# Inverse transform's first products in eight array tiles: even and odd frequencies apart, two groups per block

## The chip, the cores and the metric

The kernel runs on one core of a Trainium2 chip. The time is device microseconds from the first to the last instruction of the core, with what lies around them, as a median over repeated runs. Five engines work side by side: TensorE (PE, with PEld for its weight loads), VectorE (DVE), ScalarE (ACT), GpSimd (POOL) and SyncE (SP), which only issues DMAs here.

## The reference

```python
# x: (8, 3008, 256), filters: (1505, 256), w_in: (256, 2048), w_out: (2048, 256), all float32
X = np.fft.rfft(x, axis=1)
Y = X * (filt_r + 1j * filt_i)[None, :, :]
y = np.fft.irfft(Y, n=3008, axis=1).astype(np.float32)
x = y.reshape(8 * 3008, 256)
h = x @ w_in
out = (h * (1.0 / (1.0 + np.exp(-h))) @ w_out).astype(np.float32)
```

A filter in the frequency domain along the 3008 tokens of each of 8 batches, and then a two-layer network with a SiLU between the layers, on all 24064 tokens.

## The kernel before

**Two kinds of work share TensorE.** The network is the larger one. A batch has 48 steps: 2 halves of the tokens, 3 pairs of chunks in each half (256, 256 and 240 columns), and 8 pairs of blocks of the hidden dimension (`jp`). Both layers multiply 2x2 blocks with seven products each instead of eight. `hidden(step)` makes the first layer (products into px and pyz, combined by ScalarE and VectorE, SiLU on ScalarE), and `project(step - 1)` makes the second layer one step later, into the four accumulator banks a0 to a3 of a pair of chunks. When the last `jp` of a pair is projected, `drain` copies the accumulators out: a0 and a2 on ScalarE, a1 and a3 on VectorE; POOL then makes seven additions, and VectorE's transposes and SP's stores follow some steps later (`output`).

**The transform of batch b** is done while batch b - 1 is in the network, in pieces put between the steps (`spectral`):

- `load_x`, `sums`, `stage1` (products pa, L284, and a store to DRAM by POOL), eight times.
- `load_t2` (SP), `forward` (products pb, L307, into two banks), six groups g of frequencies.
- `multiply` (filter, VectorE, L319) and `add` (L327, L328), into tiles z of 64 real and imaginary rows for each of two banks k.
- `inverse` (products pc, L337): tile z times the table e_t, 128 columns of outputs that stand for 64 values of n and two parts. Two copies (`evac`, alternately VectorE L208 and ScalarE L210) and four stores to DRAM (L348) follow at once.
- `load_t4` (SP) and `stage3` (products pd, L368), eight groups; the first four before the batch enters the network, and the last four during its steps 9 to 18. The copies of pd make the tile y that the network reads (`tokens` forms its sums and differences).

**Who sets the order.** The schedule is written out by hand. A step has eight rounds. In each round `hidden` and `project` each issue what belongs to it, at most one product each, and then the pieces whose time has come are issued: `put(step, rnd, piece)` gives a piece its step and round, and `plan(b)` names them relative to the batch's first step (`at`). Each engine executes its own instructions in the order of issue; SP's and POOL's DMA queues too. A tile's buffer is taken again only after its last reader.

**PSUM** has eight banks: px, pyz, two banks of the pool `fps` (tag f) for all transform products of batches 1 to 7, and a0 to a3. Batch 0, whose transform runs before the network starts, uses f and a0 to a3 in a ring of six (`bank`).

The order in which `project` uses the accumulators (operand, slot of g, accumulator i, half h of its bank):

```python
PROJECT = [(A11, 0, 0, 0), (A12, 3, 1, 0), (S4, 2, 2, 0), (S1, 4, 0, 1), (S3, 5, 1, 1),
           (S2, 6, 2, 1), (A22, 7, 3, 0)]
```

Batch 0's transform, the loading of filters and tables and the rounding of the network's weights (`round_weights`, L590 to L603) make up the start, before the first network product.

Of the kernel before, what the change touches and what calls it, by code (L numbers as in the profile page):

```python
# [36 lines left out]
FP32 = mybir.dt.float32  # L40
U32 = mybir.dt.uint32
AFT = mybir.ActivationFunctionType
ALU = mybir.AluOpType
# [6 lines left out]
NS, NG = 24, 6  # L50
# [35 lines left out]
def dft_tables():  # L86

    wf = np.zeros((128, 2, 64))
    for par in range(2):
        for i, idx in enumerate(ORDER):  # L90
            ph = 2 * np.pi * (np.arange(N1) * (2 * idx + par) % 94) / 94
            for h in range(2):
                wf[64 * h:64 * h + N1, par, 2 * i] = np.cos(ph)
                wf[64 * h:64 * h + N1, par, 2 * i + 1] = -np.sin(ph)


    d = np.zeros((2, 2, 32, NS, 2, 32))
    n = np.arange(32)[:, None]
    for par in range(2):
        for i, idx in enumerate(ORDER):  # L100
            sp = 2 * idx + par
            kap = kept(sp)
            sg = np.where((kap - sp) % 94 == 0, 1.0, -1.0)
            k = np.where((kap - sp) % 94 == 0, kap, S - kap)
            th = 2 * np.pi * (n * k % S) / S
            d[par, 0, :, i, 0], d[par, 1, :, i, 0] = np.cos(th), np.sin(th)
            d[par, 0, :, i, 1], d[par, 1, :, i, 1] = -np.sin(th) * sg, np.cos(th) * sg


    e = np.zeros((4, 32, NG, 2, 2, 2, N2))  # L110
    n = np.arange(N2)[None, :]
    for g in range(NG):
        for bank in range(2):
            for j in range(4):
                s = slot_residue(g, bank, j - j % 2)
                kap = kept(slot_residue(g, bank, j))
                sg = np.where((kap - s) % N1 == 0, 1.0, -1.0)[:, None]
                k = np.where((kap - s) % N1 == 0, kap, S - kap)[:, None]
                assert ((k - s) % N1 == 0).all()
                th = 2 * np.pi * (n * k % S) / S  # L120
                e[j, :, g, bank, 0, 0], e[j, :, g, bank, 0, 1] = np.cos(th), np.sin(th)
                e[j, :, g, bank, 1, 0], e[j, :, g, bank, 1, 1] = -np.sin(th) * sg, np.cos(th) * sg


    ph = 2 * np.pi * (np.outer(np.arange(N1), np.arange(NS)) % N1) / N1
    v = np.stack([2 * np.cos(ph), -2 * np.sin(ph)], 0)

    v[0, :, 0], v[1, :, 0] = 1.0, 0.0
    wi = np.zeros((128, N1))
    for h in range(2):  # L130
        wi[64 * h:64 * h + 2 * NS] = v.transpose(0, 2, 1).reshape(2 * NS, N1) / S
    f32 = np.float32
    return (wf.astype(f32), wi.astype(f32), d.reshape(128, NS, 2, 32).astype(f32),
            e.reshape(128, NG, 2, 2, 128).astype(f32))


@with_exitstack
def kernel(
# [18 lines left out]
    def pool(name, bufs, space=None):  # L157
        kw = {} if space is None else {"space": space}
        return ctx.enter_context(tc.tile_pool(name=name, bufs=bufs, **kw))
# [5 lines left out]
    upool = pool("u", 1)  # L165
    tpool = pool("t12", 2)
    ppool = pool("p", 2)
    zpool = pool("z", 3)
    qpool = pool("q", 2)
    t4pool = pool("t4", 2)  # L170
    gpool = pool("g", 2)
# [8 lines left out]
    wf_t = cpool.tile([128, 2, 64], FP32)  # L180
    wi_t = cpool.tile([128, N1], FP32)
    d_t = cpool.tile([128, NS, 2, 32], FP32)
    e_t = cpool.tile([128, NG, 2, 2, 128], FP32)
    f_t = [cpool.tile([128, NG, 2, C], FP32, name=f"filt{i}") for i in range(2)]

    w_t = cpool.tile([128, 7, 2, NJP, 128], FP32)
# [18 lines left out]
    def evac(dst, src):  # L205
        flip[0] ^= 1
        if flip[0]:
            nc.vector.tensor_copy(out=dst, in_=src)  # L208
        else:
            nc.scalar.copy(out=dst, in_=src)  # L210
# [1 line left out]
    y = {}  # L212
    early = [0]

    def bank(b, name):

        if b > 0 or early[0] is None:
            return fps.tile([128, 2, C], FP32, name=name, tag="f")
        early[0] += 1
        k = early[0] % 6  # L220
        if k < 2:
            return fps.tile([128, 2, C], FP32, name=name, tag="f")
        return accps.tile([128, 2, C], FP32, name=name, tag=f"a{k - 2}")

    def spectral(b):

        d1 = dpool.tile([2, NS, 2, 32, C], FP32, name=f"d1_{b}", tag="d1")
        d2 = dpool.tile([2 * NS, N2, C], FP32, name=f"d2_{b}", tag="d2")
        xs, us, t2s, banks, prods, t4s = {}, {}, {}, {}, {}, {}

        def load_x(u):

# [94 lines left out]
            eng.tensor_tensor(out=z[:, 0], in0=z[:, 0], in1=pt[:, 1], op=ALU.subtract)  # L327
            eng.tensor_tensor(out=z[:, 1], in0=z[:, 1], in1=pt[:, 0], op=ALU.add)  # L328

        def inverse(g):  # L330
            zs = [z for z, _ in prods.pop(g)]
            ps = [bank(b, f"pc_{b}_{g}_{i}") for i in range(2)]
            for k in range(2):
                for ri in range(2):
                    for i in range(2):
                        rows = slice(64 * i, 64 * i + 64)
                        nc.tensor.matmul(out=ps[i][:, k, :], lhsT=e_t[rows, g, k, ri, :],  # L337
                                         rhs=zs[k][rows, ri, :], start=(ri == 0), stop=(ri == 1))
            for i in range(2):
                if b > 0 or i == 0:  # L340
                    qt = qpool.tile([128, 2, C], FP32, name=f"q_{b}_{g}_{i}", tag="q")
                else:
                    qt = opool.tile([128, 2, C], FP32, name=f"q_{b}_{g}_{i}", tag="o")
                evac(qt, ps[i])
                for p in range(2):
                    a0 = p * NS + 2 * g + 12 * i
                    queue = nc.gpsimd if b > 0 or (g == NG - 1 and i == 0) else nc.scalar
                    queue.dma_start(out=d2[a0:a0 + 2, :, :].rearrange("s n c -> n s c"),  # L348
                                    in_=qt[64 * p:64 * p + 64, :, :])

        def load_t4(g):
            t4s[g] = t4pool.tile([128, 4, C], FP32, name=f"t4_{b}_{g}", tag="t4")
            for h in range(2):
                nc.sync.dma_start(out=t4s[g][64 * h:64 * h + 2 * NS],
                                  in_=d2[:, 32 * h + 4 * g:32 * h + 4 * g + 4, :])

        def stage3(g):
            half, n0 = divmod(4 * g, 16)
# [16 lines left out]
            for h in range(2):  # L375
                evac(dst[:, :, h, n0:n0 + 4], ps[h])

        return dict(load_x=load_x, sums=sums, stage1=stage1, load_t2=load_t2, forward=forward,
                    multiply=multiply, add=add, inverse=inverse, load_t4=load_t4, stage3=stage3)

    pending = []

# [4 lines left out]
    def plan(b, part):  # L387

        at = STEPS * b

        put(at - 51, 0, part["load_x"], 0)
        put(at - 51, 0, part["load_x"], 1)
        for u in range(8):
            put(at + u - (48 if u else 49), 5, part["sums"], u)
            put(at + u - 47, 3, part["stage1"], u)
        put(at - 39, 0, part["load_t2"], 0)
        put(at - 39, 0, part["load_t2"], 1)
        for g, step in enumerate((-37, -34, -31, -28, -25, -21)):
            late = 4 if g == 4 else 0
            put(at + step, 3, part["forward"], g)  # L400
            put(at + step, 5, part["multiply"], g, 0)
            put(at + step + 1, 1, part["multiply"], g, 1)
            put(at + step + 1, 5 + late, part["add"], g, 0)
            put(at + step + 2, 1 + late, part["add"], g, 1)
            put(at + step + (3 if late else 2), 3, part["inverse"], g)
        put(at - 18, 5, part["load_t4"], 0)
        for g, step in enumerate((-16, -12, -8, -4)):
            put(at + step, 3, part["stage3"], g)
        plan_rest(b, part)

    def plan_rest(b, part):
# [85 lines left out]
    def project(step):  # L497

        pair, jp = divmod(step, NJP)
        n, g = pairs[pair][3], g_t.pop(step)  # L500
        if jp == 0:
            acc[pair] = [accps.tile([128, 2, 256], FP32, name=f"acc_{pair}_{i}", tag=f"a{i}")
                         for i in range(4)]
        last = jp == NJP - 1
        for c, k, i, h in PROJECT:

            nc.tensor.matmul(out=acc[pair][i][:, h, 0:n], lhsT=w_t[:, c, 1, jp], rhs=g[:, k, 0:n],  # L507
                             start=(jp == 0 and h == 0), stop=last, skip_group_check=True)
            if last and (h == 1 or i == 3):
                drain(pair, i)  # L510
            yield
# [118 lines left out]
    def rounded(j):  # L630
        if wide:
            round_weights(j)
        else:
            load_exact(j)


    nc.sync.dma_start(out=wf_t, in_=wf_dram.ap())
    nc.gpsimd.memset(bias_t, -896.0)
# [17 lines left out]
    for g in range(NG):  # L656
        part["forward"](g)
        if g == 0:
            load_filters(4, 2 * NG)
            nc.sync.dma_start(out=wi_t, in_=wi_dram.ap())  # L660
        if g < 3:
            weights(1 + g)
        for k in range(2):
            part["multiply"](g, k)
        for k in range(2):
            part["add"](g, k)
        if 2 <= g < NG - 1:
            rounded(g)
        if g > 0:
            part["inverse"](g - 1)  # L670
    part["inverse"](NG - 1)
    weights(4)
    part["load_t4"](0)
    for j in range(5, 9):
# [74 lines left out]
```

## Time and profile before

| what | value |
|---|---|
| median of 3 runs | 2720.2 us (2719.74 to 2721.34) |
| profiled execution, its own time | 2718.15 us |
| its span, first to last instruction | 2716.4 us |
| mean granted TensorE clock | 0.987 |
| first network product starts | 126.6 us |
| TensorE / VectorE / ScalarE / POOL busy, 0 to 127 us | 57.1 / 75.0 / 24.5 / 57.9 us |
| the same, 184 to 2717 us | 2521.2 / 1531.1 / 1049.5 / 420.2 us |
| DMA share, 0 to 127 us, and 184 to 2717 us | 0.88, 0.23 |

TensorE's busy time is that of overlapping, pipelined matmuls with modelled ends: a busy TensorE is not one at its peak, and how long a block of matmuls occupies it is read from start times. Each fp32 matmul of the code is two records of matmul and two of weight load. In a group of the profile, the first number after the bar is the group's busy time in microseconds, the second the mean of one instruction in nanoseconds, and after the second bar stands the time its engine sat idle before it, with what ended that idle time. A timeline line has start and length in microseconds.

### The profile page before, as it was taken

To read this page: it belongs to the slowest core of one execution; us is meant where nothing else is said; L and a number is where in the kernel's file an instruction comes from. 1 tells how busy PE (TensorE), PEld (TensorE's weight loads), DVE (VectorE), ACT (ScalarE), POOL (GpSimd) and SP (SyncE) were. 2 spreads that over 40 slices of the span, in tenths; PEclk is the share of its full clock that TensorE was granted. 3 is DMA by queue.
4 is the path that set the end of the run, shared out by engine and by line. 5 is a ranking of instruction groups with operands and counts; after the bars stand their busy time and mean duration, and the time that the engine had idled before them with its cause. 6 is when DMAs were issued, how large, how long until landed. Compare 5 with 4: busy or idle time off the path is not lost.

```text
span 2716.4 us, 45798 instructions
## 1 busy us (share of the span) xinstructions
PE 2626.7 (97%) x17664; PEld 2203.4 (81%) x17664; DVE 1654.5 (61%) x3494; ACT 1099.1 (40%) x2994; POOL 505.1 (19%) x738
## 2 busy tenths in 40 slices
PE   4589999999999999999999999999999999999998
PEld 1368888788887888888887888978888788898987
DVE  4786655666566665666656665566655666555554
ACT  1244344433444334444444434444344443444443
POOL 3542111211011111111201121021111111100100
PEclk9699999999999999999999999999999999999999
DMA  9733121421224211332122312133121421110000
GB/s 216 191 101 86 40 47 31 107 63 37 43 59 99 61 43 24 81 88 53 36 44 77 80 44 55 29 97 70 39 47 43 102 65 35 37 28 21 9 16 16
DMA packets 188122, 166.95 MB, mean 61 GB/s; under 512 B 122432, under 2 KB 155584, under 8 KB 187648
## 3 DMA queue, kind: packets, MB, share of 16 engines
q1 hardware_dynamic: 166296, 111.89, 18.1%
q0 software_dynamic: 16352, 47.47, 6.9%
q10 hardware_dynamic: 5256, 4.67, 0.8%
q8 instruction: 138, 2.26, 0.3%
q14 instruction: 80, 0.66, 0.1%
HBM read 88.96 MB, written 74.97 MB: 60 GB/s over the span
## 4 chain that ended last, share of the span: by engine, by line
PE 93%; DMA 3%; DVE 2%; issue 1%; ACT 1%; SPq 0%; POOL 0%; ACTq 0%; DVEq 0%
PE acc L507 41%; PE px L451 25%; PE pyz L451 18%; PE pc L337 3%; PE pd L368 2%; PE pa L284 2%; PE pb L307 2%; DMA x<-in_x_dram 1%; DVE g L422 0%; DMA filt<-in_filt_i_dram 0%; DMA raw<-in_moe_w_out_dram 0%; DVE u L267 0%; DMA e_t<-e_tbl 0%; DMA d<-q 0%; DMA t<-d 0%
## 5 line engine op out<-in xcount | busy, mean ns | idle before, releaser
L507 PE MATMUL acc<-g,w_t 128*128 128x256 f32 (+1 forms) x5376 | 1513.3, 375 | 0.4 <-DVE g L422 0.4
L507 PEld LDWEIGHTS acc<-g,w_t 128*128 128x128 f32 x5376 | 1023.0, 190 | 114.8 <-DVE g L422 0.8
L422 DVE TENSOR_TENSOR g<-pyz,abc 128x256 f32<-128x256 f32 (+1 forms) x1152 | 479.3, 416 | 543.7 <-ACT abc L472 317.2
L422 DVE TENSOR_TENSOR g<-g 128x256 f32<-128x256 f32 (+3 forms) x1152 | 613.2, 532 | 196.7 <-ACT g L455 183.5
L451 PE MATMUL px<-ty,w_t 128*128 128x256 f32 (+1 forms) x2304 | 695.6, 384 | 4.0 <-ACT abc L466 3.5
L455 ACT ACTIVATE g<-g 128x256 f32<-128x256 f32 (+1 forms) x1152 | 472.9, 411 | 232.3 <-DVE g L422 232.3
L451 PEld LDWEIGHTS px<-ty,w_t 128*128 128x128 f32 x2304 | 421.1, 190 | 128.5 <-issue 71.9
L451 PE MATMUL pyz<-y,w_t 128*128 128x256 f32 (+1 forms) x1536 | 456.3, 379 | 1.7 <-DVE g L422 1.7
L422 POOL TENSOR_TENSOR s<-s 128x256 f32<-128x256 f32 (+1 forms) x329 | 263.0, 816 | 976.0 <-DVE s L525 952.8
L451 PEld LDWEIGHTS pyz<-y,w_t 128*128 128x128 f32 x1536 | 282.2, 190 | 46.9 <-DVE g L422 8.1
L466 ACT COPY abc<-px 128x256 f32<-128x256 f32 (+1 forms) x384 | 141.3, 368 | 375.1 <-PE px L451 375.1
L455 ACT ACTIVATE g<-px 128x256 f32<-128x256 f32 (+1 forms) x384 | 145.8, 380 | 301.2 <-PE px L451 301.2
L472 ACT COPY abc<-px 128x256 f32<-128x256 f32 (+1 forms) x384 | 142.9, 372 | 285.3 <-PE px L451 284.9
L348 POOL DMA_DIRECT2D d<-q x170 | 100.6, 598 | 755.7 <-DVE q L208 750.4
L451 PE MATMUL px<-y,w_t 128*128 128x256 f32 (+1 forms) x768 | 226.6, 377 | 3.6 <-ACT g L455 2.6
L451 PE MATMUL pyz<-ty,w_t 128*128 128x256 f32 (+1 forms) x768 | 226.7, 377 | 0.3 <-DVE g L422 0.3
L451 PEld LDWEIGHTS px<-y,w_t 128*128 128x128 f32 x768 | 144.6, 190 | 22.5 <-issue 3.0
L451 PEld LDWEIGHTS pyz<-ty,w_t 128*128 128x128 f32 x768 | 145.2, 190 | 19.5 <-DVE g L422 3.2
L459 ACT COPY abc<-px 128x256 f32<-128x256 f32 (+1 forms) x384 | 134.1, 349 | 1.3 <-PE px L451 1.3
L289 POOL DMA_DIRECT2D d<-t x124 | 63.5, 516 | 294.6 <-ACT abc L472 276.8
L208 DVE COPY y<-pd 128x376 f32<-128x376 f32 x64 | 51.4, 807 | 94.8 <-PE pd L368 94.8
L337 PE MATMUL pc<-z,e_t 64*128 64x256 f32 x768 | 102.7, 410 | 4.0 <-DMA e_t<-e_tbl 2.6
(52 smaller groups left out, 1316.4 us busy)
## 6 DMA issues: line engine op xcount, KB each, us to landing
t<-d SPq DMA_DIRECT2D x96, 256.0 KB, 3.9
t<-d SPq DMA_DIRECT2D x128, 192.0 KB, 3.7
d<-t POOLq DMA_DIRECT2D x124, 192.0 KB, 3.0
d<-q POOLq DMA_DIRECT2D x170, 128.0 KB, 2.6
out_dram<-o SPq DMA_DIRECT2D x636, 32.0 KB, 1.8
x<-in_x_dram SPq DMA_DIRECT2D x120, 128.0 KB, 3.1
x<-in_x_dram SPq DMA_DIRECT2D x120, 60.0 KB, 3.0
raw<-in_moe_w_in_dram SPq DMA_DIRECT2D x16, 256.0 KB, 4.8
```

What stands on the lines that cost most here:

```text
L284: nc.tensor.matmul(out=ps[h][64 * par:64 * par + 64], lhsT=wf_t[rows, par], rhs=ut[rows, par], start=True, stop=True)
L289: nc.gpsimd.dma_start(out=d1[par].rearrange("s p n c -> (s p) n c")[:, 4 * u:4 * u + 4, :], in_=t1[64 * par:64 * par + 2 * NS].rearrange(" ...
L307: nc.tensor.matmul(out=ps[k][32 * j:32 * j + 32, ri, :], lhsT=d_t[rows, 4 * g + at, ri, :], rhs=t2[rows, at, :], start=True, stop=True)
L337: nc.tensor.matmul(out=ps[i][:, k, :], lhsT=e_t[rows, g, k, ri, :], rhs=zs[k][rows, ri, :], start=(ri == 0), stop=(ri == 1))
L348: queue.dma_start(out=d2[a0:a0 + 2, :, :].rearrange("s n c -> n s c"), in_=qt[64 * p:64 * p + 64, :, :])
L422: eng.tensor_tensor(out=out, in0=in0, in1=in1, op=op)
L451: nc.tensor.matmul(out=out, lhsT=w_t[:, c, 0, jp], rhs=rhs, start=start, stop=True, skip_group_check=True)
L455: nc.scalar.activation(out=g[:, k, 0:n], in_=g[:, k, 0:n] if src is None else src, func=AFT.Silu)
L459: nc.scalar.copy(out=sums[:, 0, 0:n], in_=xo)
L466: nc.scalar.copy(out=sums[:, 1, 0:n], in_=xo)
L472: nc.scalar.copy(out=sums[:, 2, 0:n], in_=xo)
L507: nc.tensor.matmul(out=acc[pair][i][:, h, 0:n], lhsT=w_t[:, c, 1, jp], rhs=g[:, k, 0:n], start=(jp == 0 and h == 0), stop=last, skip_group ...
```

## The change

- The table of `inverse` now gives, for each of the four quarters j of 32 rows of z, 64 outputs: 32 values of n, and two parts. Quarters 0 and 2 hold the even frequencies and 1 and 3 the odd ones. The products of a quarter go to a bank of its own, and the sum and the difference of an even and an odd bank give n and n + 32.
- A matmul thus has 32 rows and 64 columns, an eighth of the array. A group has 16 of them instead of 8.
- For batches 1 to 7 one call of `inverse` makes two groups. It stands in round 7 of three steps (-32, -24, -16), those in which a pair of chunks ends, and takes the accumulator banks a0 and a1 for the even halves, and both f banks for the odd ones. In the step after, `project` begins with the product into a2.
- `even` copies an even half on ScalarE; `rows` makes sum and difference on VectorE, and issues the stores, one per group and half with runs of 2 KB, where there were two with runs of 1 KB. `load_t4` reads runs of 1 KB, where it read 4 KB.
- The table e_t has half the size, there are four z buffers instead of three, and q tiles are twice as large. `forward` and what follows it, and `stage3`, have other steps.
- Batch 0 makes single groups (`inverse_rows`), with the same split.

```diff
-    zpool = pool("z", 3)
+    zpool = pool("z", 4)
...
-    e_t = cpool.tile([128, NG, 2, 2, 128], FP32)
+    e_t = cpool.tile([128, NG, 2, 2, 64], FP32)
...
+        if b > 0 and spare is not None:
+            return accps.tile([128, 2, C], FP32, name=name, tag=f"a{spare}")
...
-        d2 = dpool.tile([2 * NS, N2, C], FP32, name=f"d2_{b}", tag="d2")
+        d2 = dpool.tile([2 * NS, 32, 2, C], FP32, name=f"d2_{b}", tag="d2")
...
-        def inverse(g):
-            zs = [z for z, _ in prods.pop(g)]
-            ps = [bank(b, f"pc_{b}_{g}_{i}") for i in range(2)]
-            for k in range(2):
+        def inverse(g, n=1):
+
+            ps = [bank(b, f"pc_{b}_{g}_{j}", j // 2 if j % 2 == 0 else None) for j in range(4)]
+            for a in range(n):
+                zs = [z for z, _ in prods.pop(g + a)]
                 for ri in range(2):
-                    for i in range(2):
-                        rows = slice(64 * i, 64 * i + 64)
-                        nc.tensor.matmul(out=ps[i][:, k, :], lhsT=e_t[rows, g, k, ri, :],
-                                         rhs=zs[k][rows, ri, :], start=(ri == 0), stop=(ri == 1))
...
+                    for j in range(4):
+                        rows = slice(32 * j, 32 * j + 32)
+                        for k in range(2):
+
+                            nc.tensor.matmul(out=ps[j][64 * k:64 * k + 64, a, :],
+                                             lhsT=e_t[rows, g + a, k, ri, :], rhs=zs[k][rows, ri, :],
+                                             start=(a == 0 and ri == 0), stop=(ri == 1),
+                                             skip_group_check=True)
+            halves[g] = ps, []
+
+        def even(g, i, n=1):
...
+            nc.scalar.copy(out=qt[:, 0:n, 1], in_=halves[g][0][2 * i][:, 0:n])
+            halves[g][1].append(qt)
+
+        def rows(g, i, n=1):
+
+            ps, qts = halves[g]
+            qt = qts[i]
+            for h, op in ((0, ALU.add), (1, ALU.subtract)):
+                nc.vector.tensor_tensor(out=qt[:, 0:n, h], in0=qt[:, 0:n, 1],
+                                        in1=ps[2 * i + 1][:, 0:n], op=op)
+            for a in range(n):
+                a0 = 8 * (g + a) + 4 * i
+                queue = nc.gpsimd if b > 0 or (g == NG - 1 and i == 0) else nc.scalar
+                queue.dma_start(out=d2[a0:a0 + 4].rearrange("a n h c -> (a n) h c"), in_=qt[:, a])
...
-                                  in_=d2[:, 32 * h + 4 * g:32 * h + 4 * g + 4, :])
+                                  in_=d2[:, 4 * g:4 * g + 4, h, :])
...
-        for g, step in enumerate((-37, -34, -31, -28, -25, -21)):
-            late = 4 if g == 4 else 0
+        for g, step in enumerate((-38, -35, -29, -27, -22, -19)):
...
-            put(at + step + (3 if late else 2), 3, part["inverse"], g)
-        put(at - 18, 5, part["load_t4"], 0)
-        for g, step in enumerate((-16, -12, -8, -4)):
-            put(at + step, 3, part["stage3"], g)
...
+        for g, step in ((0, -32), (2, -24), (4, -16)):
+
+            put(at + step, 7, part["inverse"], g, 2)
+            put(at + step, 7, part["even"], g, 0, 2)
+            put(at + step + 1, 0, part["even"], g, 1, 2)
+            put(at + step + 1, 3, part["rows"], g, 0, 2)
+            put(at + step + 1, 6, part["rows"], g, 1, 2)
+        put(at - 14, 5, part["load_t4"], 0)
+        for g, (step, rnd) in enumerate(((-12, 3), (-9, 3), (-6, 3), (-3, 3))):
+            put(at + step, rnd, part["stage3"], g)
...
+        order = PROJECT[2:3] + PROJECT[0:2] + PROJECT[3:] if jp == 0 else PROJECT
+        for c, k, i, h in order:
...
+    def inverse_rows(part, g):
+        part["inverse"](g)
+        for i in range(2):
+            part["even"](g, i)
+            part["rows"](g, i)
```

More of the change, by code (lines that the diff above doesn't have):

```diff
@@ L107, in dft_tables @@
             d[par, 0, :, i, 1], d[par, 1, :, i, 1] = -np.sin(th) * sg, np.cos(th) * sg
-    e = np.zeros((4, 32, NG, 2, 2, 2, N2))
-    n = np.arange(N2)[None, :]
+    e = np.zeros((4, 32, NG, 2, 2, 2, 32))
+    n = np.arange(32)[None, :]
     for g in range(NG):
@@ L118, in dft_tables @@
                 k = np.where((kap - s) % N1 == 0, kap, S - kap)[:, None]
-                assert ((k - s) % N1 == 0).all()
+                assert ((k - s) % 94 == (0 if j % 2 == 0 else N1)).all()
                 th = 2 * np.pi * (n * k % S) / S
@@ L122, in dft_tables @@
                 e[j, :, g, bank, 1, 0], e[j, :, g, bank, 1, 1] = -np.sin(th) * sg, np.cos(th) * sg
-    ph = 2 * np.pi * (np.outer(np.arange(N1), np.arange(NS)) % N1) / N1
-    v = np.stack([2 * np.cos(ph), -2 * np.sin(ph)], 0)
-    v[0, :, 0], v[1, :, 0] = 1.0, 0.0
     wi = np.zeros((128, N1))
     for h in range(2):
-        wi[64 * h:64 * h + 2 * NS] = v.transpose(0, 2, 1).reshape(2 * NS, N1) / S
+        for i in range(NS):
+            s = slot_residue(i // 4, i % 2, i // 2 % 2 * 2)
+            ph = 2 * np.pi * ((2 * np.arange(N1) + h) * s % 94) / 94
+            wi[64 * h + 2 * i] = 2 * np.cos(ph) / S if s else 1.0 / S
+            wi[64 * h + 2 * i + 1] = -2 * np.sin(ph) / S if s else 0.0
     f32 = np.float32
     return (wf.astype(f32), wi.astype(f32), d.reshape(128, NS, 2, 32).astype(f32),
-            e.reshape(128, NG, 2, 2, 128).astype(f32))
+            e.reshape(128, NG, 2, 2, 64).astype(f32))
 @with_exitstack
@@ L213, with bank @@
     early = [0]
-    def bank(b, name):
+    def bank(b, name, spare=None):
+        if b > 0 and spare is not None:
+            return accps.tile([128, 2, C], FP32, name=name, tag=f"a{spare}")
         if b > 0 or early[0] is None:
@@ L227, in spectral @@
         d1 = dpool.tile([2, NS, 2, 32, C], FP32, name=f"d1_{b}", tag="d1")
-        d2 = dpool.tile([2 * NS, N2, C], FP32, name=f"d2_{b}", tag="d2")
-        xs, us, t2s, banks, prods, t4s = {}, {}, {}, {}, {}, {}
+        d2 = dpool.tile([2 * NS, 32, 2, C], FP32, name=f"d2_{b}", tag="d2")
+        xs, us, t2s, banks, prods, halves, t4s = {}, {}, {}, {}, {}, {}, {}
         def load_x(u):
@@ L328, in add @@
             eng.tensor_tensor(out=z[:, 1], in0=z[:, 1], in1=pt[:, 0], op=ALU.add)
-        def inverse(g):
-            zs = [z for z, _ in prods.pop(g)]
-            ps = [bank(b, f"pc_{b}_{g}_{i}") for i in range(2)]
-            for k in range(2):
+        def inverse(g, n=1):
+            ps = [bank(b, f"pc_{b}_{g}_{j}", j // 2 if j % 2 == 0 else None) for j in range(4)]
+            for a in range(n):
+                zs = [z for z, _ in prods.pop(g + a)]
                 for ri in range(2):
-                    for i in range(2):
-                        rows = slice(64 * i, 64 * i + 64)
-                        nc.tensor.matmul(out=ps[i][:, k, :], lhsT=e_t[rows, g, k, ri, :],
-                                         rhs=zs[k][rows, ri, :], start=(ri == 0), stop=(ri == 1))
[L339 to L349, printed above, removed]
@@ new lines, in even @@
+        def even(g, i, n=1):
+            if b > 0 or i == 0:
+                qt = qpool.tile([128, 2, 2, C], FP32, name=f"q_{b}_{g}_{i}", tag="q")
+            else:
+                qt = opool.tile([128, 1, 2, C], FP32, name=f"q_{b}_{g}_{i}", tag="o")
+            nc.scalar.copy(out=qt[:, 0:n, 1], in_=halves[g][0][2 * i][:, 0:n])
[10 more added lines that the diff above has]
+                queue.dma_start(out=d2[a0:a0 + 4].rearrange("a n h c -> (a n) h c"), in_=qt[:, a])
@@ L378, in spectral @@
         return dict(load_x=load_x, sums=sums, stage1=stage1, load_t2=load_t2, forward=forward,
-                    multiply=multiply, add=add, inverse=inverse, load_t4=load_t4, stage3=stage3)
+                    multiply=multiply, add=add, inverse=inverse, even=even, rows=rows, load_t4=load_t4, stage3=stage3)
     pending = []
@@ L402, in plan @@
             put(at + step + 1, 1, part["multiply"], g, 1)
-            put(at + step + 1, 5 + late, part["add"], g, 0)
-            put(at + step + 2, 1 + late, part["add"], g, 1)
-            put(at + step + (3 if late else 2), 3, part["inverse"], g)
-        put(at - 18, 5, part["load_t4"], 0)
-        for g, step in enumerate((-16, -12, -8, -4)):
-            put(at + step, 3, part["stage3"], g)
+            put(at + step + 1, 5, part["add"], g, 0)
+            put(at + step + 2, 1, part["add"], g, 1)
+        for g, step in ((0, -32), (2, -24), (4, -16)):
[7 more added lines that the diff above has]
+            put(at + step, rnd, part["stage3"], g)
         plan_rest(b, part)
@@ L501, in project @@
         if jp == 0:
-            acc[pair] = [accps.tile([128, 2, 256], FP32, name=f"acc_{pair}_{i}", tag=f"a{i}")
-                         for i in range(4)]
+            acc[pair] = {}
         last = jp == NJP - 1
-        for c, k, i, h in PROJECT:
+        order = PROJECT[2:3] + PROJECT[0:2] + PROJECT[3:] if jp == 0 else PROJECT
+        for c, k, i, h in order:
+            if i not in acc[pair]:
+                acc[pair][i] = accps.tile([128, 2, 256], FP32, name=f"acc_{pair}_{i}", tag=f"a{i}")
             nc.tensor.matmul(out=acc[pair][i][:, h, 0:n], lhsT=w_t[:, c, 1, jp], rhs=g[:, k, 0:n],
@@ L669 @@
         if g > 0:
-            part["inverse"](g - 1)
-    part["inverse"](NG - 1)
+            inverse_rows(part, g - 1)
+    inverse_rows(part, NG - 1)
     weights(4)
```

## The prediction

> **What bounds the kernel now.** I read the page first for the engine that the end hangs on (engine shares, then the chain that ended last), and the groups for the edited lines.
>
> ```profile
> PE 2626.7 (97%) x17664; PEld 2203.4 (81%) x17664; DVE 1654.5 (61%) x3494; ACT 1099.1 (40%) x2994; POOL 505.1 (19%) x738
> PE 93%; DMA 3%; DVE 2%; issue 1%; ACT 1%; SPq 0%; POOL 0%; ACTq 0%; DVEq 0%
> ```
>
> TensorE carries 93% of the chain; the chain's line shares give the inverse's first products (pc, L337) 3%. A microsecond of TensorE stream saved is a microsecond off the end, if nothing else becomes late. The groups, shapes kept apart (busy us, mean ns):
>
> ```profile
> L422 DVE TENSOR_TENSOR g<-pyz,abc 128x256 f32<-128x256 f32 x768 | 323.8, 422 | 358.5 <-ACT abc L472 199.7 <-PE pyz L451 148.0 <-PE acc L507 0.2
> L337 PE MATMUL pc<-z,e_t 64*128 64x256 f32 x768 | 102.7, 410 | 4.0 <-DMA e_t<-e_tbl 2.6 <-DVE z L327 1.3
> L307 PE MATMUL pb<-t,d_t 64*32 64x256 f32 x1536 | 58.8, 397 | 40.8 <-DVE work L596 20.1 <-DMA t<-d 20.0 <-DVE work L590 0.5
> L208 DVE COPY q<-pc 128x512 f32<-128x512 f32 x48 | 33.2, 691 | 86.3 <-PE pc L337 86.2
> L210 ACT COPY q<-pc 128x512 f32<-128x512 f32 x48 | 28.1, 586 | 136.6 <-PE pc L337 102.4 <-PE pb L307 21.5 <-issue 4.9
> ```
>
> Matmul durations overlap, so a block's price is read from start times. TensorE's timeline at a pc, a pb and a pd block of batch 4 (start us, us, then the operation):
>
> ```profile
> 1208.91 0.59 PE L507 MATMUL acc<-g,w_t 128*128 128x256 f32 x2
> 1209.43 2.00 PE L337 MATMUL pc<-z,e_t 64*128 64x256 f32 x16
> 1211.36 0.70 PE L451 MATMUL px<-ty,w_t 128*128 128x256 f32 x2
> ```
> ```profile
> 1194.33 0.60 PE L507 MATMUL acc<-g,w_t 128*128 128x256 f32 x2
> 1194.85 1.09 PE L307 MATMUL pb<-t,d_t 64*32 64x256 f32 x32
> 1195.88 0.70 PE L451 MATMUL px<-ty,w_t 128*128 128x256 f32 x2
> ```
> ```profile
> 1181.49 1.15 PE L368 MATMUL pd<-wi_t,t 48*64 48x47 f32 x64
> ```
>
> Undisturbed pairs start 0.43 us apart, 0.216 per record. The pc block pushes the stream back by 1211.36 - 1208.91 - 0.43 = 2.02 us, the pb block by 1.12. Every one of the 42 blocks of batches 1 to 7 is alike (mean 2.016, all within 0.02). pc has 16 records in two row tiles: 16/2 x 0.216 = 1.73, and 0.29 of entering and leaving. pb has 32 records in eight tiles: 32/8 x 0.216 = 0.86, and 0.25. So eight tiles at once do work here.
>
> **What the Trainium skill says.** "TensorE: Matmul & The Clock Gate", section "Measured speedup vs the span model", gives 3.07x for four row tiles and 10.6x for sixteen: packing goes on gaining beyond two tiles. The pb block agrees (eight at a time). "TensorEngine Tiling (Array Packing)", section "Key Properties", says that a change of tiling mode drains the engine: the 0.25 to 0.29 us per block agree. Its "Gotcha 1: PSUM Pressure" says that different row tiles can't use one bank at once; no run here shows the penalty, and the change gives each of the four row tiles its own bank.
>
> **The change, part by part.**
>
> *Products.* Before, a group is 8 matmuls, 16 records. After, it is 16 matmuls of 32 rows x 64 columns, 32 records in eight tiles (4 row x 2 column), and a block holds two groups: 64/8 x 0.216 = 1.73 us + 0.27 (between pb's and pc's entry) = 2.00 us, against 2 x 2.016 = 4.03. Batches 1 to 7 have 21 such blocks: **21 x 2.03 = -42.7 us.** No 32x64 tile is in the trace. Could its weight loads be too slow? pd loads 64 columns 64 times in the 1.08 us to the next product (1182.57) into four tiles, so one tile takes at most 68 ns per load, under the 216 of a wave. Bounds: 1.98 per block (-43), and four at a time (first rival).
>
> *Place of the block.* It stands at the end of a step in which a pair of chunks ends, and takes two accumulator banks, a0 and a1, between their drain and the next pair's first product. TensorE must find them drained. From the timeline at such a step's end:
>
> ```profile
> 1290.61 0.56 ACT L525 COPY s<-acc 128x480 f32<-128x480 f32 x1 [0.35 <-PE acc L507]
> 1290.63 0.65 DVE L525 COPY s<-acc 128x480 f32<-128x480 f32 x1
> 1291.34 0.42 ACT L455 ACTIVATE g<-g 128x256 f32<-128x256 f32 x1
> 1291.68 0.59 PE L451 MATMUL px<-y,w_t 128*128 128x256 f32 x2
> 1292.11 0.59 PE L507 MATMUL acc<-g,w_t 128*128 128x256 f32 x2
> ```
>
> a1's drain on VectorE ends 1291.28, 0.40 us before the next step starts (0.37 to 0.53 over all pairs), so the block waits for nothing. The reordered first product (S4, into a2) needs a2's drain (ended 1291.17) and the silu that ends 1291.76; it starts at 1292.11: 0.35 spare (0.30 with 240 columns), also at boundaries without a block: cost 0. a0 is wanted by the fourth pair after the block, a1 by the sixth: 1.4 and 2.3 us after the first pair starts. ScalarE copies a0's half from 0.1 us on (0.59), then the step's px (0.37), which can start at 0.7, then a1's half (0.59); the halves are out at 0.7 and 1.7: spare 0.7 and 0.6. Cost 0; if both covers failed, TensorE would wait (second rival).
>
> *Sums.* Per two groups 2 VectorE and 2 ScalarE copies become 2 ScalarE copies (same 0.59) and 4 VectorE operations of 128x512, at the copy's 0.69: 2.76 against 1.38, +29 us of VectorE over 21 blocks. They stand in rounds 3 and 6 of the next step, two at 1.38 us each. VectorE's own work there is 2.9 us of 6.05, with a gap of about 1.7 before round 4's combine and 1.3 before round 7's. They fit; the chain to the next product has 1.1 to 1.2 us of slack in every step. Cost 0; POOL's 7 additions (5.9 us) slow SBUF-only VectorE work beside them, already so before.
>
> *DMAs.* 192 stores of 128 KB become 96 of 256 KB in 2 KB runs, so POOL issues 85 fewer at 0.6 us. Those after a block queue on POOL behind the 7 additions and behind VectorE's sums; nobody on POOL is urgent. Counted from the start of the last block's step (6.05 us a step, 2.0 for the block), the sums end at 14.3, two issues at 15.5, landing at about 18; load_t4(0) is reached on SP at 18 (a wait there holds x loads and output stores behind it) and lands 3.9 later (t2's 1 KB runs; t4's long ones took 3.7); stage3(0) comes at 28.7: 7 us spare. forward(0) is one step earlier: its t2 load is issued at 1179.46, lands about 1184, and forward would start about 1188.7: 4.7 us spare. Cost 0.
>
> *Start (batch 0, first main product at 126.6 us).* DMA is 84 to 108% busy from 20 to 80 us; e_t shrinks from 1536 to 768 KB. Landing took 9.0 us; d_t, of 768 KB, took 5.9; at the windows' 196 to 225 GB/s it is 3.5 to 4 us: -3.5 for the filters at 71.5, which start the stretch bound by VectorE. Then groups 1 to 4: each swaps one 0.69 copy for four sums of 128x256 (0.42): +1.0, plus a wait, as i=1's ScalarE copy (0.36) stands behind i=0's DMA issue (0.6), which waits for i=0's sums: +1.0; the fourth z buffer removes a 0.7 us wait for pc: 4 x 1.3 = +5.2. Fewer ACT issues (11 x 0.6) help only groups 4 and 5: 0 taken. Net **+1.7**; bounds -4 (all of it hidden) and +9 (nothing saved).
>
> *Sum:* -42.7 + 1.7 = -41.0. The profiled execution (2718.15 us, span 2716.4) becomes 2677.2; the median shown stands 2.05 above it, so 2679.2.
>
> **Rivals.**
> 1. *Four tiles at a time* (two column tiles of one row group don't overlap): 16 x 0.216 + 0.27 = 3.73 per block, -6.3 + 1.7: 2715.6, no change. For: no such tile shown. Against: pb's four column tiles share row groups and overlap.
> 2. *Hand-over wait*: right tiles, but TensorE waits 0.5 to 1 us per block for a0, a1 or delayed silus: 2690 to 2700 (0.7: 2694). For: margins of 0.3 to 0.7 us. Against: they are positive everywhere.
> 3. *Slower*: 32-row tiles run two at a time as pc's do now: 32 x 0.216 + 0.27 = 7.18, +3.15 x 21 + 1.7: 2788. It decides below 64 x 0.216 / (4.03 - 0.27 - 0.08) = 3.8 tiles. For: twice the records. Against: pb.
> That the split saves nothing at all is rival 1.
>
> **How the numbers follow.** Forecast 0.79, rival 1 0.05, rival 2 0.12, rival 3 0.04. 0.2% (5.4 us) is about what a measurement can tell. Forecast, rival 2 and 0.02 of rival 1 are faster: 0.93; the rest of rival 1 same: 0.03; slower 0.04. Range 2669 (start hidden, entry shorter, 4 us for error) to 2698 (most of rival 2).
>
> **What would show it.** pc x64 blocks, 21 of them, pushing the stream by 2.0 us; 3.7 or 7.2 names rivals 1 or 3. PE idle before acc or pc on ACT or DVE names rival 2. First main product near 128 us. The sums near 690 ns, POOL d<-q x85. Wrong if the blocks cost 2.0 and the time is not 35 to 47 us lower.

## The result, and the profile after

The changed kernel takes 2707.96 us (median of 4 runs, 2706.44 to 2708.59), against 2719.97 us before (2719.03 to 2721.34). The ratio is 0.9955, with a 95% interval of 0.9937 to 0.9972. It is 12 us faster, where 41 were forecast, and lies above the forecast range. The profiled execution has a span of 2705.5 us, 10.9 less than before.

The page's engine shares and its chain:

```profile
PE 2600.5 (96%) x18432; PEld 2162.2 (80%) x18432; DVE 1675.9 (62%) x3554; ACT 1100.6 (41%) x3000; POOL 448.3 (17%) x653
PE 84%; DVE 9%; DMA 3%; SPq 1%; ACT 1%; issue 1%; POOL 0%; DVEq 0%; ACTq 0%
```

The shares of busy time have hardly moved, but VectorE holds 9% of the chain where it held 2%. TensorE is now released by VectorE in many places. First the block itself, on TensorE's timeline (start us, us, operation):

```profile
1280.56 0.59 PE L479 MATMUL pyz<-y,w_t 128*128 128x256 f32 x2
1281.08 1.98 PE L348 MATMUL pc<-z,e_t 32*64 32x256 f32 x64
1282.99 0.70 PE L479 MATMUL px<-y,w_t 128*128 128x256 f32 x2
```

64 records push the stream back by 1282.99 - 1280.56 - 0.43 = 2.00 us. Over all 21 blocks it is 42.0 us, against 84.7 in 42 blocks before: the 42.7 us forecast are there. The groups (busy us, mean ns) have the new instructions at about the prices used:

```profile
L348 PE MATMUL pc<-z,e_t 32*64 32x256 f32 x1536 | 60.2, 411 | 2.9 <-DVE q L367 1.4 <-DVE z L335 0.8 <-POOL z L336 0.5
L367 DVE TENSOR_TENSOR q<-q,pc 128x512 f32<-128x512 f32 x84 | 57.2, 681 | 1.4
L372 POOL DMA_DIRECT2D d<-q x85 | 46.2, 547 | 57.9 <-DVE q L367 55.1 <-issue 2.8
L359 ACT COPY q<-pc 128x512 f32<-128x512 f32 x42 | 24.7, 589 | 21.3 <-PE pc L348 21.3
```

Now TensorE's waits from 190 us on (who waited for whom: us in total, times, longest). Of before, all there was:

```profile
PE pd L368 <- DMA t<-d: 0.4, 1, 0.4
```

After:

```profile
PE pyz L479 <- DVE g L450: 15.3, 33, 1.0
PE pd L391 <- DMA t<-d: 1.8, 4, 1.0
PE acc L538 <- DVE g L450: 0.4, 1, 0.4
```

This view counts a part of the loss. More complete is the excess of each start-to-start distance between two neighbouring network records over 0.216 us (0.203 with 240 columns), worked out from the start times in the trace: 37.3 us before, 67.2 after, **29.9 more** (distances more than 30 ns over). With 2.8 more at the pd blocks and the first product at 126.56 us instead of 126.64, the sum is -42.7 + 29.9 + 2.8 - 0.1 = -10.1 of the span's -10.9. Of the other 0.8, the pa blocks take 0.4 less, and what follows the last product 0.3.

The excess is not all waiting. The second network record after a transform block, or after a wait, comes about 0.1 us late. The change takes away 21 blocks, and with them 2.1 us of this small loss. So the waits themselves have grown by some 2 us more than the 29.9, and a block taken away has brought 0.1 us more than its push.

Where the waits are is seen by sorting them by the place in the batch. Per batch (seen from the next batch's first step, and with the late record after each wait), the largest are 1.3 us in step -18, 0.8 in -25, 0.6 in -28, 0.5 in -34, and 0.4 in each of -37 and -17. Only 0.4 in -30, 0.3 in -14 and 0.1 in each of -31 and -22 stand in a step with sums or behind one. Step -18 on TensorE and on VectorE:

```profile
1320.61 0.59 PE L479 MATMUL px<-ty,w_t 128*128 128x256 f32 x2
1321.05 0.59 PE L538 MATMUL acc<-g,w_t 128*128 128x256 f32 x2
1322.62 0.70 PE L479 MATMUL pyz<-y,w_t 128*128 128x256 f32 x2 [0.97 <-DVE g L450]
```
```profile
1318.77 0.77 DVE L568 STREAM_TRANSPOSE o<-s 128x256 f32<-128x256 f32 x2
1319.46 0.65 DVE L450 TENSOR_TENSOR ty<-y 128x512 f32<-128x512 f32 x1
1320.15 0.88 DVE L450 TENSOR_TENSOR ty<-y,ty 128x256 f32<-128x256 f32 x2
1320.95 0.68 DVE L327 TENSOR_TENSOR z<-pb,filt 128x512 f32<-128x512 f32 x1
1321.55 0.68 DVE L327 TENSOR_TENSOR p<-pb,filt 128x512 f32<-128x512 f32 x1
1322.14 0.42 DVE L450 TENSOR_TENSOR g<-pyz,abc 128x256 f32<-128x256 f32 x1
```

The plan puts the transposes of an output, the tokens of the next pair of chunks and a multiply in one round: 3.4 us of VectorE work without a gap. Behind them stands the combine that reads the y half of pyz (start 1322.14, end 1322.56). The product S4, which adds to that half (`mm(yo, S4, ...)`), starts at 1322.62. pyz is one bank with one buffer. Each half is written, read by VectorE and written again within a few rounds; a late reader stops TensorE.

### The profile page after: what moved, and what is told of

The parts are those of the page before. It is cut to its first block, busy times and chain, and to the rows that moved or that the text cites. A ratio compares the mean times of both kernels' runs of the same rounds, so it can differ in the third digit from the quotient of the medians.

```text
span 2705.5 us, 47315 instructions
## 1 busy us (share of the span) xinstructions
PE 2600.5 (96%) x18432; PEld 2162.2 (80%) x18432; DVE 1675.9 (62%) x3554; ACT 1100.6 (41%) x3000; POOL 448.3 (17%) x653
## 4 chain that ended last, share of the span: by engine, by line
PE 84%; DVE 9%; DMA 3%; SPq 1%; ACT 1%; issue 1%; POOL 0%; DVEq 0%; ACTq 0%
PE acc L538 37%; PE px L479 22%; PE pyz L479 17%; DVE g L450 3%; PE pd L391 3%; PE pa L292 2%; PE pb L315 2%; PE pc L348 2%; DMA t<-d 1%; DVE q L367 1%; DVE ty L450 1%; DVE p L327 1%; DVE o L568 1%; DVE z L327 1%; DMA x<-in_x_dram 1%
## 5 line engine op out<-in xcount | busy, mean ns | idle before, releaser
L479 PE MATMUL pyz<-y,w_t 128*128 128x256 f32 (+1 forms) x1536 | 461.9, 382 | 18.7 <-DVE g L450 16.9
L391 PEld LDWEIGHTS pd<-wi_t,t 48*64 48x64 f32 x4096 | 70.7, 140 | 37.6 <-issue 21.9
L315 PE MATMUL pb<-t,d_t 64*32 64x256 f32 x1536 | 62.2, 411 | 38.2 <-DMA t<-d 37.2
```

The source lines that it names most:

```text
L315: nc.tensor.matmul(out=ps[k][32 * j:32 * j + 32, ri, :], lhsT=d_t[rows, 4 * g + at, ri, :], rhs=t2[rows, at, :], start=True, stop=True)
L391: nc.tensor.matmul(out=ps[h][c0:c0 + 64, cb, i, :], lhsT=t4s[g][rows, i, 128 * cb + c0:128 * cb + c0 + 64], rhs=wi_t[rows, :], start=True, ...
L479: nc.tensor.matmul(out=out, lhsT=w_t[:, c, 0, jp], rhs=rhs, start=start, stop=True, skip_group_check=True)
```

## The experiments

In all of them, *waits* is the excess described above, from step 10 of the first batch on: 23.3 us before, 52.6 after, 29.3 more. In it, 19.8 us of before and 17.7 of after are only the late second record after a block; without these the waits are 3.5 and 35.0.

**One collision taken away.** The transposes and stores of the third pair of chunks go from step -18 to -20.

```diff
-    stores = (((10, 1), (10, 5)), ((19, 5), (20, 1)), ((30, 1), (30, 5)), ((34, 1), (34, 5)),
+    stores = (((10, 1), (10, 5)), ((19, 5), (20, 1)), ((28, 1), (28, 5)), ((34, 1), (34, 5)),
```

> The changed kernel with one edit: the transposes and stores of each batch's third pair of chunks are placed in rounds 1 and 5 of step 28 (seen from the next batch: -20) instead of step 30 (-18). Theory A (TensorE waits in the network because VectorE's reads of pyz come late wherever several extra VectorE pieces are placed in one round): step -18 holds tokens, two transposes and a multiply in round 1; the trace after shows 8.3 us of TensorE waits there and 1.8 in step -17 over seven batches. Without the transposes tokens and the multiply remain, as in step -34 (0.36 us per batch, 2.5 us): 7.6 us less, 2700.4 us. Theory B (the sums on VectorE are what costs): no sums are near these steps, so within 1 us of the changed kernel, 2708.

Measured: 2699.38 us, 8.6 less than the changed kernel's median, where theory A had 7.6 and theory B at most 1; the waits are 44.8. Steps -18 and -17 lost 11.6 us in seven batches and now lose 3.7. No product, sum or copy was touched: the place of four transposes per batch is worth 8 us.

**The sums all but left out.**

```diff
-                nc.vector.tensor_tensor(out=qt[:, 0:n, h], in0=qt[:, 0:n, 1],
-                                        in1=ps[2 * i + 1][:, 0:n], op=op)
+                nc.vector.tensor_tensor(out=qt[:, 0:n, 1, 0:8], in0=qt[:, 0:n, 1, 0:8],
+                                        in1=ps[2 * i + 1][:, 0:n, 0:8], op=op)
...
-                queue.dma_start(out=d2[a0:a0 + 4].rearrange("a n h c -> (a n) h c"), in_=qt[:, a])
+                queue.dma_start(out=d2[a0:a0 + 4].rearrange("a n h c -> (a n) h c"),
+                                in_=qt[:, a, 1:2, :].to_broadcast([128, 2, C]))
```

> The changed kernel with the sums cut to 8 of 512 columns per group and half (the rest of the sums and differences is left out, and the even half is stored twice), so that VectorE's work for the sums all but goes while places, copies, blocks and stores stay. Theory A (the places of multiplies, additions and transposes cost the time): only the waits that follow the sums go, in steps -30, -22 and -14: 3.5 us in seven batches, 2704.5 us. Theory B (the sums' 1.38 us more per group pair, 29 us in all, are what TensorE waits for): some 25 us less, 2683 us.

Measured: 2696.76 us, 11.2 less. That is three times theory A's 3.5, and less than half of theory B's 25. The waits are 46.0, so the sums account for 6.7 of the 29.3 added: in seven batches 2.9 us in step -30, 1.9 in -14, 1.1 in -31 and 0.8 in -22. Theory A's 3.5 left out the late record after each wait. The pd blocks push 1.2 us less, and the first network product starts at 123.2 instead of 126.6. These 3.4 us are mostly not the price of the sums in batch 0: the table d_t landed 1.7 us earlier in this execution, before any sum, and the last filter 2.6 us earlier (67.1 against 69.7). About 0.8 us is left for the sums. TensorE's two largest waits from 190 us on are still there:

```profile
PE pyz L479 <- DVE g L450: 14.6, 28, 1.0
PE pd L391 <- DMA t<-d: 1.1, 3, 0.7
```

**The new places without the tiles.** The kernel before, with the changed kernel's steps for forward, multiply, add, load_t4 and stage3, and nothing else. `inverse` stays one group per block and two steps behind its `forward`, so it does not stand where the changed kernel has it.

```diff
-        for g, step in enumerate((-37, -34, -31, -28, -25, -21)):
-            late = 4 if g == 4 else 0
+        for g, step in enumerate((-38, -35, -29, -27, -22, -19)):
+            late = 0
...
-        put(at - 18, 5, part["load_t4"], 0)
-        for g, step in enumerate((-16, -12, -8, -4)):
+        put(at - 14, 5, part["load_t4"], 0)
+        for g, step in enumerate((-12, -9, -6, -3)):
```

> The kernel before with the changed kernel's steps for forward, multiply, add, load_t4 and stage3, and nothing else changed (products in two row tiles, one group per block, copies). Theory A: the new steps bring the collisions with tokens and transposes without the eight tiles; the trace after shows 29.3 us more of TensorE waits than before, of which 3.5 follow the sums: about 25 us slower than before, 2745 us (2735 to 2752). Theory B: the steps are harmless, within 3 us of before, 2720.

Measured: 2749.31 us, 29.7 slower than before (ratio 1.0111, 1.0098 to 1.0125). The waits rise from 23.3 to 46.6, with the same largest places (8.7 us in step -18, 6.7 in -25, 4.0 in -28). That is 23.3 us, about what the changed kernel has without its sums: 29.3 - 6.7 = 22.6. The late records after blocks left out, the two kernels also agree step by step, in seven batches: 8.7 and 9.1 us in -18, 6.0 and 6.0 in -25, 4.0 and 4.3 in -28, 3.2 and 3.2 in -34, 2.5 and 2.5 in each of -37 and -17. The plan alone costs them. Another 5.4 us are forward's waits for a bank, which this mixture alone has:

```profile
PE pyz L451 <- DVE g L422: 14.2, 28, 1.0
PE pb L307 <- DVE q L208: 5.4, 7, 0.8
PE pd L368 <- DMA t<-d: 1.3, 3, 0.7
```

**The work spread over the steps.** The changed kernel, with multiplies and additions given their own places, outputs moved to free steps, and the second sum pair a step later.

```diff
+        for g, step, mul, plus in (
+                (0, -38, ((-38, 5), (-37, 1)), ((-37, 5), (-36, 1))),
+                (1, -35, ((-35, 5), (-34, 5)), ((-33, 1), (-33, 5))),
+                (2, -29, ((-29, 5), (-28, 1)), ((-28, 5), (-27, 1))),
+                (3, -27, ((-27, 5), (-26, 1)), ((-25, 1), (-25, 5))),
+                (4, -22, ((-22, 5), (-21, 1)), ((-21, 5), (-20, 1))),
+                (5, -19, ((-19, 5), (-18, 5)), ((-17, 1), (-17, 5)))):
...
-            put(at + step + 1, 6, part["rows"], g, 1, 2)
+            put(at + step + 2, 1, part["rows"], g, 1, 2)
...
-    stores = (((10, 1), (10, 5)), ((19, 5), (20, 1)), ((30, 1), (30, 5)), ((34, 1), (34, 5)),
+    stores = (((10, 1), (12, 5)), ((18, 5), (19, 1)), ((26, 1), (28, 5)), ((34, 1), (34, 5)),
```

> The changed kernel with its VectorE pieces spread: at most one multiply, or the tokens, or a sum pair in the gap of rounds 1 to 4 and at most one multiply or the tokens in that of rounds 5 and 6; the transposes of the first three pairs of chunks moved to steps without other pieces; the second sum pair one step later, in round 1. Blocks, products, sums and stores stay. Theory A: nearly all of the 29.3 us of added waits go, and some of those that the kernel before had (2 us in step -25): 2680 us (2676 to 2688). Theory B: the same VectorE work is done, so the waits stay: 2700 to 2708.

Measured: 2687.56 us (ratio to before 0.9885, 0.9871 to 0.9898). The waits are 20.7: all that the change had added is gone, though VectorE does the same work. The time lies at the upper end of theory A's range and not at its 2680, because two pieces became late instead. The pd blocks push 4.6 us more than before (75.8 against 71.2), and forward(4), at -22, has a wait in its middle in all seven batches (10.3 us in all). On TensorE, and on VectorE at the same time:

```profile
1284.34 0.62 PE L315 MATMUL pb<-t,d_t 64*32 64x256 f32 x2
1285.87 1.09 PE L315 MATMUL pb<-t,d_t 64*32 64x256 f32 x30 [0.91 <-issue]
```
```profile
1283.70 0.77 DVE L573 STREAM_TRANSPOSE o<-s 128x256 f32<-128x256 f32 x2
1284.39 1.37 DVE L367 TENSOR_TENSOR q<-q,pc 128x512 f32<-128x512 f32 x2
```

The sums that end at 1285.76 are the last readers of the f bank in which pb goes on at 1285.87. The profile says "issue", as it has no releaser for this wait.

**The two late pieces mended.** The second sum pair of the block at -24 goes back to step -23, round 6, and stage3 stands in other steps.

```diff
-            put(at + step + 2, 1, part["rows"], g, 1, 2)
+            put(at + step + (1 if g == 2 else 2), 6 if g == 2 else 1, part["rows"], g, 1, 2)
...
-        for g, (step, rnd) in enumerate(((-12, 3), (-9, 3), (-6, 3), (-3, 3))):
+        for g, (step, rnd) in enumerate(((-11, 3), (-8, 3), (-6, 3), (-3, 3))):
```

> The spread kernel with two places mended. In its trace forward(4) lost 10.3 us in seven batches, as its bank f is freed by the second sum pair of the block at -24, which stood only two rounds ahead: that pair goes back to step -23, round 6. And stage3 lost 2.5 us to load_t4, late on SP behind 16 stores: the four stage3 go to steps -11, -8, -6, -3. Theory A: both go, at a price of 1 us for the sum pair: 2687.6 - 10.3 - 2.5 + 1 = 2675.8 us (2673 to 2680). Theory B (what is left is the sums' own cost, wherever they stand): no change, 2687.

Measured: 2672.86 us (2670.49 to 2673.55), ratio to before 0.983 (0.9816 to 0.9843). It beats both kernels, and is 46.1 us faster than before in the same session: with the VectorE pieces in other places, the whole forecast saving of 41 arrives. The time is just below the range expected, as stage3 had lost more than the 2.5 us put down for it: its blocks push 70.2 us, 5.6 less than in the spread kernel. The pb blocks are back at 1.12 us each. The chain has TensorE at 93% again, and one wait of TensorE is left from 190 us on:

```profile
PE 93%; DVE 2%; DMA 2%; SPq 1%; issue 1%; ACT 1%; POOL 0%; ACTq 0%; DVEq 0%
```
```profile
PE acc L543 <- DVE g L455: 0.4, 1, 0.4
```

The waits are 21.6, of which 17.7 are the late records after blocks. The sums take as long as in the changed kernel (84 of them, 680 ns each, against 681).

**How much room VectorE has in a step.** The kernel before, with reductions without use.

```diff
+        def idle(n):
+            for _ in range(n):
+                nc.vector.tensor_reduce(out=warm, in_=f_t[0][:, 0].rearrange("p k c -> p (k c)"), op=ALU.add, axis=mybir.AxisListType.X)
+        for step, rnd, n in ((-13, 5, 2), (-11, 5, 3), (-5, 1, 3), (-3, 1, 4)):
+            put(at + step, rnd, idle, n)
```

> The kernel before with extra VectorE work in otherwise free steps of each of seven batches: a reduction of 128x512 (about 0.65 us, its result unused), two in round 5 of step -13, three in round 5 of -11, three in round 1 of -5, four in round 1 of -3. Theory A (VectorE has two gaps per step: 1.5 us ahead of round 7's combine, whose read of pyz holds the next step's second product, and some 2.2 us ahead of round 4's): no wait after -13, 0.5 us after -11, 0 to 0.1 in -5, 0.5 in -3, each batch: 7 x 1.0 = 7 us, 2727 us. Theory B (VectorE, 61% busy, has room for 2.6 us in any step, as its chain to the next step's products has 1.1 us of slack): no waits, 2720.

Measured: 2727.22 us, 8.3 slower (ratio 1.0033, 1.0021 to 1.0045). One reduction takes 683 ns:

```profile
L411 DVE TENSOR_REDUCE warm<-filt 128x1 f32<-128x512 f32 x84 | 57.4, 683 | 1.9
```

Waits added per batch: none after two in round 5 (1.37 us), 0.53 us after three (2.05); 0.06 after three in round 1, 0.78 after four (2.73). So the gap ahead of round 4's combine holds about 2.0 us, and what goes beyond is paid in full by TensorE (0.68 us more work, 0.72 more wait). If that holds for the gap ahead of round 7's combine too, where one dose lies beyond it, that gap is about 1.5 us. VectorE is idle for over a third of the time all the while. In all the waits are 9.6 us more than before in the profiled execution, and the medians differ by 8.3, where theory A had 7. A dose in the second gap, on VectorE and TensorE:

```profile
1430.68 2.84 DVE L411 TENSOR_REDUCE warm<-filt 128x1 f32<-128x512 f32 x4
1433.44 0.40 DVE L427 TENSOR_TENSOR g<-pyz,abc 128x240 f32<-128x240 f32 x1
```
```profile
1432.81 0.57 PE L512 MATMUL acc<-g,w_t 128*128 128x240 f32 x2
1433.89 0.67 PE L456 MATMUL pyz<-y,w_t 128*128 128x240 f32 x2 [0.51 <-DVE g L427]
```

## Why the prediction was wrong

- **Products: right.** 21 blocks at 2.00 us, forecast 2.00; -42.7 us, forecast -42.7. Rivals 1 and 3 (four or two tiles at a time) are out.
- **Place of the block: right.** TensorE never waits for a0 or a1 and 0.4 us in all for an operand of acc. Rival 2 is out as it was put: there are waits of TensorE on VectorE, but none at the hand-over.
- **The step that failed: "the chain to the next product has 1.1 to 1.2 us of slack in every step".** It is under *Sums*. I took the slack of the last combine of a step, whose reader is the second layer's product four rounds later. In the trace of before that is 1.22 us (median over the steps), so the figure was read rightly. The combines of rounds 4 and 7, which read the y half of pyz, have less, since the bank has one buffer. In the kernel before, at the end of a step (timeline of both engines):

```profile
1291.88 0.42 DVE L422 TENSOR_TENSOR g<-pyz,abc 128x256 f32<-128x256 f32 x1
1292.54 0.60 PE L451 MATMUL pyz<-y,w_t 128*128 128x256 f32 x2
```

  The combine ends at 1292.30 and the next writer of the bank starts at 1292.54: 0.24 us, which is also the median over the steps; for round 4's combine it is 0.70. So the sums, priced at nothing, cost 6.7 us of waits in the network. A part of them may be due to POOL, whose slowing of VectorE the prediction names and gives no cost: ahead of the first sum pair in the step after the block shown above, two subtractions on VectorE take 1.64 us beside POOL's additions, and the same two a step later 0.87. No run separates the two.
- **The larger part of the failure is a term left out, 22.6 of the 29.3 us.** The change moves `forward` and with it every multiply and addition. The prediction prices the move for forward's load alone and gives VectorE's instructions no line in the sum, which puts their move at nothing without a reason. So it does not see three pieces meet in step -18, nor the meetings in -38, -34, -29, -28 and -26. The third and the first experiment show that this term is the plan's, not the tiles'.
- **DMAs: nearly right.** No wait of TensorE falls on the stores. load_t4 had no 7 us to spare, as 16 output stores issue on SP ahead of it (in the trace after from 1347.8 to 1355.8 us, then the load, and stage3 at 1359.7 finds a part of its data missing). The pd blocks push 2.8 us more than before, nearly all of it in this first stage3.
- **Start: net forecast +1.7, measured -0.1.** The first product of equal starts scatters by up to 2.6 us, so one pair of executions does not settle this. The landing of wi_t, the load behind the last filter, parts the two terms. It comes at 72.5, 75.6 and 74.6 us in the three traces with the start of before and at 68.1 to 70.2 in the four with the changed start and its sums: 4.9 earlier on average, forecast 3.5. From there to the first product it takes 53.6 to 54.6 us in the three and 56.6 to 58.3 in the four: 3.3 more on average, forecast 5.2. Both terms have the forecast sign, and the second was taken too large.
- The sentence on what would make it wrong ("the blocks cost 2.0 and the time is not 35 to 47 us lower") is what came.

## What to carry to other kernels

A saving on the bounding engine arrives only if no other engine has become late. When a change moves work, list for every moved instruction the queue that it enters and which instruction behind it has the next deadline; the busy share of that engine (61% here) did not show it. A deadline is set by the next *writer* of the operand's buffer as well as by the reader of the result: here, with one buffer of pyz in PSUM, the writer came first (0.24 us, against 1.2). And measure the gap, by putting work in it, before filling it.

## What the runs showed that I had not expected

Eight 32x64 tiles run as eight 64x32 tiles do: 64 records in 2.00 us with entering and leaving, although each weight load has twice the columns (140 against 111 ns). In the trace after, eight records of the block start within 0.05 us of each other, the next eight 0.27 us behind them, and every further eight 0.216 us behind the ones before.

In `forward`'s blocks both row tiles write to one bank at the same time, each to its own quarter of the partitions (`slot_source` gives bank k both), and their 32 records still push the stream by only 1.12 us. So these runs give no sign that two row tiles must keep to different banks; with the change's own tiles that was not tried.
